# Two pairs of score bursts two gathers later, and one batch's transposes one unit at a step

## The chip, the cores and the metric

The kernel runs on one core of a Trainium2 chip. The metric is the device time of one execution in microseconds. The engines are named as in the profile: PE is TensorE, PEld its weight loads, DVE is VectorE, ACT is ScalarE, POOL is GpSimd and SP is SyncE, which here only issues DMAs.

## What is computed

A talking-heads attention over 8 batches, 12 heads, 448 positions and 64 features a head, and behind it a feed-forward layer with a squared ReLU:

```python
scores = scale * np.matmul(q, k.transpose(0, 1, 3, 2))        # q, k, v: (8, 12, 448, 64)
scores = np.einsum('bhij,hg->bgij', scores, w_pre)             # heads mixed before the softmax
attn = np.exp(scores - np.max(scores, axis=-1, keepdims=True))
attn = attn / (np.sum(attn, axis=-1, keepdims=True) + 1e-09)
attn = np.einsum('bhij,hg->bgij', attn, w_post)                # heads mixed after it
x = np.matmul(attn, v)                                         # to (8*448, 768)
...
h = np.maximum(x @ w_in, 0.0)                                  # w_in: (768, 2048)
out = h * h @ w_out                                            # w_out: (2048, 768)
```

## The kernel before

**Tiles and steps.** A tile is ten query positions of one batch with all twelve heads, 120 rows, by 448 keys. A batch has 45 tiles, so the main loop has 360 steps and a few more at its end; in step `i` the tile `steps[i]` is mixed (`mix`) and the tile four steps back is finished (`unmix`). Step 45 is the first tile of batch 1, step 90 that of batch 2.

**Stages of a tile.** `mix` multiplies the gathered scores G (120 rows) with a matrix that mixes heads (m_ps, L438); ScalarE takes the exponential (e, L442) with its row sums; VectorE takes reciprocals (rc, L449), and GpSimd scales the second mixing matrix with them (pn, L452). `unmix` multiplies e with pn, which also transposes (at_ps, L467 and L471), and VectorE copies the result (at, L473). After every fifteen tiles `av_unit` multiplies with v (ot_ps, L229 and L236). The feed-forward layer of a batch (h_ps at L283, hr, h; o_ps at L328, osb) is cut into units in the list `filler`, and `fill` puts them between the other work so that TensorE has something to do.

**Scores and gathers.** Scores are computed by heads, but a tile needs all heads of ten positions together. So a *burst* (`score_burst`) computes the scores of one *block* of 128 query positions for three of the six head pairs: six matmuls (s_ps, L377) into six PSUM banks, then six copies into a tile `S`, four on ScalarE (L387) and two on VectorE (L389). Two bursts fill a block. `S` has two buffers, which the blocks take in turn. A DMA issued by SyncE (`gather`, L406) then moves the rows of a tile out of S into one of twelve buffers G. Gathers run ten steps ahead of their use. A burst's copies overwrite the block two back, so they wait for the last gather out of that one; a gather waits for the copies of its block.

**When bursts are issued.** `FIRST[b][blk]` is the first tile that counts as block `blk`'s. When the gather of that tile plus n has been issued, and n is in `BURSTS[b][blk]`, one of the two bursts of the *following* block is issued:

```python
first = BURSTS[b2][blk2]
if nxt < len(blocks) and t2 - FIRST[b2][blk2] in first:
    x = first.index(t2 - FIRST[b2][blk2])
    score_burst(*blocks[nxt], [3 * x, 3 * x + 1, 3 * x + 2])
```

`FIRST` is (0, 13, 26, 39) for batches from 1 on. So `BURSTS[1][1]` = [5, 8] places the bursts of batch 1's third block behind the gathers of its tiles 18 and 21, which are issued in steps 53 and 56, and `BURSTS[2][0]` = [5, 8] those of batch 2's second block behind the gathers of its tiles 5 and 8, in steps 85 and 88.

**Transposes.** The next batch's q and k are staged by DMAs and transposed on TensorE. A `turn_unit` transposes two head pairs of q or k: 28 small matmuls (tr_ps, L214) into two PSUM banks and two copies on VectorE (L216). A batch needs three units for k and then three for q; `TURN` gives the step of each, counted from the first step of the batch before.

**What sets the order.** The order on TensorE and GpSimd is that of the program. A scheduler orders VectorE and ScalarE. Every PSUM tile is one of eight banks, taken in turn, so a matmul that opens a tile waits until the tile eight before it has been read. Weights, q, k and v are loaded by DMAs that GpSimd issues at set steps (L89, L250, L254, L267, L273).

Of the kernel before, what the change touches and what calls it, by code (L numbers as in the profile page):

```python
# [14 lines left out]
B, H, S, D = 8, 12, 448, 64  # L15
# [17 lines left out]
BURSTS = {0: ([4, 8], [5, 8])}  # L33
for _b in range(1, B):
    STARTS[_b], FIRST[_b], BURSTS[_b] = (0, 128, 256, 384), (0, 13, 26, 39), ([5, 8], [5, 8], [6], [2, 4])
GATHERS_AT = 2
HALF = H // 2
TT = 15
TQ = TT * IQ
LAG = 4  # L40
AHEAD = 10
SCALE = 1.0 / 8.0
TURN = {0: (21, 21, 21, 25, 25, 25), 1: (24, 24, 24, 28, 28, 28), B: (2 + LAG,) * 3 + (17 + LAG,) * 3}
KQ_LATER = {1: (26, 28, 37, 41), B: (22, 25, 28, 31)}
V_LATER = {1: (30, 32, 34), B: (34, 37, 40)}
KQ_AT = {1: (4, 7, 10, 12), 2: (49, 51, 53, 55)}
# [9 lines left out]
def kernel(  # L56
# [161 lines left out]
    def turn_units(b):  # L218
        return [(250, lambda u=u, w=w: turn_unit(b, w, u)) for w in (1, 0) for u in range(NPAIR // 2)]
# [145 lines left out]
    def score_burst(b, blk, pairs):  # L365

        if (b, blk) not in Sb:
            Sb[(b, blk)] = work.tile([P, H, S], BF16, name="S", tag="S", bufs=2)
        sb = Sb[(b, blk)]
        q0 = STARTS[b][blk]  # L370
        got = []
        for p in pairs:
            for hh in range(2):
                rs = slice(64 * hh, 64 * hh + 64)
                ps = bank("s_ps")
                if blk < 3:
                    nc.tensor.matmul(ps[:, 0:S], lhsT=qTs[b][rs, p, q0:q0 + P], rhs=kTs[b][rs, p, :],  # L377
                                     start=True, stop=True)
                got.append((2 * p + hh, ps))
            for c in range(2 if blk == 3 else 0):  # L380
                for hh in range(2):
                    rs = slice(64 * hh, 64 * hh + 64)
                    nc.tensor.matmul(got[2 * p + hh][1][64 * c:64 * c + 64, 0:S], lhsT=qTs[b][rs, 3 * c + p, q0:S],  # L383
                                     rhs=kTs[b][rs, 3 * c + p, :], start=True, stop=True)
        for h, ps in got:
            if h % 2 == 0 or (b < 3 and h in ((1, 3) if blk == b == 0 else (3, 9))):
                nc.scalar.copy(out=sb[:, h, :], in_=ps[:, 0:S])  # L387
            else:
                nc.vector.tensor_copy(out=sb[:, h, :], in_=ps[:, 0:S])  # L389
# [91 lines left out]
    def at_step(i, unit):  # L481
        timed.setdefault(i, []).append(unit)
# [12 lines left out]
    with tc.manual_schedule(engines={PE, POOL}):  # L495
# [40 lines left out]
        for i in range(-1, end):  # L536
# [9 lines left out]
            if s0:  # L546
                b, t = s0
                if t == 0:
                    if b + 1 < B:
                        for x, u in enumerate(turn_units(b + 1)):  # L550
                            at_step(i + TURN.get(b, TURN[B])[x], u)
            early = [x for x in bounds if x > i]
# [22 lines left out]
            if i < 2:  # L575
                score_burst(0, 0, [2 + 2 * i, 3 + 2 * i])
            for _ in range(2 if i >= GATHERS_AT else 0):
                if ahead[0] > min(max(i + AHEAD, FIRST[0][1] - 1), len(steps) - 1):
# [47 lines left out]
```

## Time and profile before

| | |
|---|---|
| median of three timed runs | 588.79 us (588.3 to 590.7) |
| profiled execution | 584.89 us |
| its span, first to last instruction | 583.1 us |
| granted TensorE clock | 0.999 |
| busy: PE, PEld | 561.5, 362.6 us |
| busy: DVE, ACT, POOL | 398.5, 378.4, 377.7 us |
| DMAs of the gathers (L406 and L409) | 312 and 98 |

Times in the profile count from the first instruction. A row of a timeline gives the start, the length, engine, line, operation, the tile written and those read, the shape and the count; in brackets stands the idle time of the engine before it and what ended that. A row of the waits gives the total, the times and the longest. TensorE's matmuls overlap in the pipeline, so a group's next start is a better measure of its cost than its length.

### The profile page before, as it was taken

The page shows a single profiled execution, that of the slowest core. Times are in us where ns is not written, and L with a number is a line of the kernel's source. Part 1 is how long each engine was busy: PE and PEld are TensorE (multiplying, and loading weights), DVE is VectorE, ACT ScalarE, POOL GpSimd, SP SyncE. Part 2 cuts the span into 40 slices and gives each one's busy share as a digit, 9 for nine tenths or more (in the row PEclk, how much of TensorE's full clock was granted, in tenths as well). Part 3 has the DMA queues.
Part 4 walks back from the last instruction along what each step waited for, and adds up shares of the span by engine and source line. Part 5 has one row for each costly group of instructions (what it writes and reads, how often), then busy time and mean ns, then how long its engine had stood idle before and what let it go on. Part 6 is the DMA issues. An engine that isn't in the chain of part 4 may idle for free.

```text
span 583.1 us, 18427 instructions
## 1 busy us (share of the span) xinstructions
PE 561.5 (96%) x6735; PEld 362.6 (62%) x6735; DVE 398.5 (68%) x979; ACT 378.4 (65%) x1090; POOL 377.7 (65%) x844
## 2 busy tenths in 40 slices
PE   4999989989999999999999999999999999999996
PEld 2677767656566566566565665666665665666554
DVE  7748848868676777866877678767877668655011
ACT  3747968678876567864876558775777548862410
POOL 6566985575877448774778547785578447774830
PEclk9999999999999999999999999999999999999999
DMA  9999999696578764796559855687544865422113
GB/s 130 153 192 172 189 200 180 135 200 161 103 120 148 144 126 89 126 154 141 101 102 140 152 126 97 121 142 157 112 73 69 145 130 101 88 46 55 29 27 82
DMA packets 84043, 72.28 MB, mean 124 GB/s; under 512 B 18768, under 2 KB 80496, under 8 KB 83952
## 3 DMA queue, kind: packets, MB, share of 16 engines
q0 software_dynamic: 37856, 33.04, 36.9%
q1 hardware_dynamic: 45514, 37.86, 30.3%
q8 instruction: 53, 0.87, 0.6%
q10 hardware_dynamic: 582, 0.21, 0.2%
q14 instruction: 38, 0.31, 0.1%
HBM read 47.28 MB, written 11.01 MB: 100 GB/s over the span
## 4 chain that ended last, share of the span: by engine, by line
PE 90%; DMA 4%; ACT 3%; issue 1%; POOL 1%; DVE 1%; ACTq 0%; POOLq 0%; SPq 0%
PE o_ps L328 25%; PE h_ps L283 24%; PE m_ps L438 11%; PE at_ps L467 10%; PE ot_ps L229 5%; PE s_ps L377 5%; PE m_ps L424 4%; DMA G<-S 3%; PE tr_ps L214 2%; PE ot_ps L236 2%; PE at_ps L471 2%; ACT e L442 1%; PE s_ps L383 1%; ACT S L387 1%; DMA kst<-in_k_dram 1%
## 5 line engine op out<-in xcount | busy, mean ns | idle before, releaser
L442 ACT ACTIVATE e<-m_ps 120x448 bf16<-120x448 f32 x360 | 196.0, 551 | 85.2 <-PE m_ps L438 46.2
L473 DVE CAST at<-at_ps 128x480 bf16<-128x480 f32 (+1 forms) x360 | 206.2, 592 | 63.4 <-PE at_ps L471 48.1
L452 POOL TENSOR_SCALAR pn<-post,rc 120x120 bf16<-120x120 bf16 (+1 forms) x340 | 122.1, 369 | 142.4 <-DVE rc L449 77.1
L283 PE MATMUL h_ps<-xt,w 128*128 128x448 bf16 (+2 forms) x960 | 165.8, 315 | 0.4 <-ACT e L442 0.2
L328 PE MATMUL o_ps<-w,h 128*128 128x384 bf16 x768 | 138.7, 326 | 0.1
L438 PE MATMUL m_ps<-G,pre 120*120 120x448 bf16 (+1 forms) x340 | 121.4, 358 | 4.1 <-ACT S L387 3.0
L467 PE MATMUL at_ps<-pn,e 120*128 120x120 bf16 x1080 | 115.8, 216 | 2.7 <-ACT S L387 2.5
L283 PEld LDWEIGHTS <-w 128*128 128x128 bf16 x960 | 83.4, 98 | 53.4 <-issue 4.2
L467 PEld LDWEIGHTS <-e 120*128 120x128 bf16 x1080 | 85.9, 98 | 47.4 <-ACT S L387 5.1
L295 POOL TENSOR_TENSOR h<-hr 128x384 bf16<-128x384 f32 (+1 forms) x128 | 103.0, 805 | 12.9 <-ACT hr L289 11.4
L328 PEld LDWEIGHTS <-h 128*128 128x128 bf16 x768 | 73.0, 98 | 47.9 <-issue 4.9
L289 ACT ACTIVATE hr<-h_ps 128x448 f32<-128x448 f32 (+2 forms) x136 | 71.9, 530 | 44.8 <-PE h_ps L283 37.3
L387 ACT CAST S<-s_ps 128x448 bf16<-128x448 f32 x177 | 82.2, 550 | 14.6 <-PE s_ps L377 9.2
L389 DVE CAST S<-s_ps 128x448 bf16<-128x448 f32 x141 | 79.8, 614 | 4.8 <-DMA G<-S 4.0
L442 ACT ACTIVATION_READ_ACCUMULATOR e<-m_ps 120x1 f32 x360 | 75.6, 210 | 0.0
L337 DVE COPY osb<-o_ps 128x384 f32<-128x384 f32 x54 | 30.1, 557 | 57.8 <-PE o_ps L328 57.6
L449 DVE RECIPROCAL rc<-sm 120x1 f32<-120x1 f32 (+1 forms) x192 | 31.1, 162 | 42.3 <-ACT e L442 30.9
L438 PEld LDWEIGHTS <-pre 120*120 120x120 bf16 (+1 forms) x340 | 44.9, 132 | 21.4 <-issue 12.3
L242 ACT CAST xt<-ot_ps 128x450 bf16<-128x450 f32 (+1 forms) x48 | 25.6, 534 | 26.5 <-PE ot_ps L236 26.0
L455 POOL TENSOR_TENSOR en<-e,rc 120x128 bf16<-120x128 bf16 (+1 forms) x112 | 42.3, 378 | 0.0
L229 PE MATMUL ot_ps<-at,v 128*64 128x150 bf16 x864 | 41.5, 229 | 0.0
L471 PE MATMUL at_ps<-post,en 120*128 120x120 bf16 x181 | 39.1, 216 | 0.0
(63 smaller groups left out, 494.6 us busy)
## 6 DMA issues: line engine op xcount, KB each, us to landing
G<-S SPq DMA_DIRECT2D x276, 105.0 KB
out_dram<-osb POOLq DMA_DIRECT2D x48, 192.0 KB, 4.5
kst<-in_k_dram POOLq DMA_DIRECT2D x14, 336.0 KB, 7.3
qst<-in_q_dram POOLq DMA_DIRECT2D x14, 336.0 KB, 5.7
G<-S SPq DMA_DIRECT2D x70, 52.5 KB
v<-in_v_dram POOLq DMA_DIRECT2D x8, 384.0 KB, 8.6
w<-in_moe_w_in_dram POOLq DMA_DIRECT2D x6, 512.0 KB, 10.3
w<-in_moe_w_out_dram POOLq DMA_DIRECT2D x8, 384.0 KB, 8.7
```

The costliest lines, as they stand in the source:

```text
L229: nc.tensor.matmul(ps[64 * hh:64 * hh + 64, TQ * y:TQ * y + TQ], lhsT=vts[b % 2][:, g, r, :], rhs=at[:, r, g, :, :].rearrange("p t i -> p ...
L283: nc.tensor.matmul(ps[:, n * j:n * j + n], lhsT=w1[f // 8][:, c2, f % 8 * 128:f % 8 * 128 + 128], rhs=xts[b][:, c2, n0:n1], start=(c2 == 0 ...
L289: nc.scalar.activation(out=hr[:, 0:k * n], in_=ps[:, 0:k * n], func=ACT.Relu)
L295: eng.tensor_tensor(out=dst[:, :, x - o:y - o], in0=hr[:, :, x - n0:y - n0], in1=hr[:, :, x - n0:y - n0], op=ALU.mult)
L328: nc.tensor.matmul(ps[:, 0:384], lhsT=lhsT, rhs=w2[ft // 4][:, ft % 4, nt * 384:(nt + 1) * 384], start=(ft == 0), stop=(ft == FT - 1))
L387: nc.scalar.copy(out=sb[:, h, :], in_=ps[:, 0:S])
L389: nc.vector.tensor_copy(out=sb[:, h, :], in_=ps[:, 0:S])
L438: nc.tensor.matmul(ps[0:n, 0:S], lhsT=m[0:n, 0:n], rhs=Gs.pop(s)[0:n, :], start=True, stop=True)
L442: nc.scalar.activation(out=e[0:n, x, :], in_=ps[0:n, 0:S], func=ACT.Exp, scale=SCALE, accum_out=sm[0:n, x:x + 1])
L452: nc.gpsimd.tensor_scalar(out=esb[(b, t - z)][1][0:rows, :], in0=(post_gi if fused else post)[0:rows, :], scalar1=rc[0:rows, z:z + 1], sca ...
L467: nc.tensor.matmul(ps[:, RG * r:RG * r + RG], lhsT=e[0:n, tl % 2, P * r:P * r + P], rhs=pn[0:n, :], start=True, stop=True)
L473: nc.vector.tensor_copy(out=ats[(b, third)][:, 0:k, :, tl, :], in_=ps[:, 0:k * RG].rearrange("p (r g i) -> p r g i", r=k, i=IQ))
```

## The change

Three entries of tables change; no operation is added or removed.

```diff
 for _b in range(1, B):
     STARTS[_b], FIRST[_b], BURSTS[_b] = (0, 128, 256, 384), (0, 13, 26, 39), ([5, 8], [5, 8], [6], [2, 4])
+BURSTS[1] = ([5, 8], [7, 10], [6], [2, 4])
+BURSTS[2] = ([7, 10], [5, 8], [6], [2, 4])
...
-TURN = {0: (21, 21, 21, 25, 25, 25), 1: (24, 24, 24, 28, 28, 28), B: (2 + LAG,) * 3 + (17 + LAG,) * 3}
+TURN = {0: (20, 22, 23, 24, 26, 27), 1: (24, 24, 24, 28, 28, 28), B: (2 + LAG,) * 3 + (17 + LAG,) * 3}
```

The bursts of batch 1's third block move behind the gathers of tiles 20 and 23 (steps 55 and 58), and those of batch 2's second block behind the gathers of tiles 7 and 10 (steps 87 and 90). The six transposing units of batch 1, which stood three by three in steps 21 and 25, go one each into steps 20, 22, 23, 24, 26 and 27. The two added lines shift every later line by two: L438 before is L440 after. The feed-forward units, which fill what is left of each step, move by a unit here and there in steps 20 to 27; from batch 2's third block on the order on every engine is as before, and GpSimd's and SyncE's orders are as before throughout.

## The prediction

> **What bounds the kernel now.** I read the first part of the page, then the windows, then the chain and the waits, and last the timelines of TensorE around each wait that the change can reach.
>
> ```profile
> PE 561.5 (96%) x6735; PEld 362.6 (62%) x6735; DVE 398.5 (68%) x979; ACT 378.4 (65%) x1090; POOL 377.7 (65%) x844
> ...
> DMA  9999999696578764796559855687544865422113
> ...
> PE 90%; DMA 4%; ACT 3%; issue 1%; POOL 1%; DVE 1%; ACTq 0%; POOLq 0%; SPq 0%
> ```
> ```profile
> 48.00:54.00 6.00, 4.89 (x132) 3.92 (x131) 5.20 (x18) 3.69 (x14) 3.60 (x9) 1.00 0.84 170
> 84.00:90.00 6.00, 3.37 (x42) 2.42 (x42) 2.52 (x7) 2.80 (x8) 5.01 (x11) 1.00 1.33 197
> 90.00:104.00 14.00, 14.00 (x205) 11.06 (x203) 11.76 (x37) 11.69 (x39) 7.26 (x19) 1.00 0.84 175
> ```
> ```profile
> 240.00:300.00 60.00, 59.68 (x747) 37.77 (x746) 44.38 (x107) 41.12 (x119) 43.31 (x99) 1.00 0.69 125
> 480.00:540.00 60.00, 60.00 (x652) 38.72 (x650) 38.91 (x93) 38.18 (x111) 38.78 (x89) 1.00 0.38 74
> ```
> The columns of a window are length, then busy us of TensorE, its weight loads, VectorE, ScalarE and GpSimd, then granted clock, DMA share and GB/s. TensorE is busy 561.5 of 583.1 us and carries 90% of the chain. From 240 us on it fills its windows (59.68 and 60.00 of 60), and the next engine, VectorE, has 15 us to spare in one of them. So a microsecond of TensorE idling that goes in the first 140 us should arrive whole at the end, unless something takes it back before then. The DMA row is what could: up to 102 us (seven slices of 14.6 us) the DMA engines are busy nine tenths or more. All of the change lies inside the first 140 us.
>
> ```profile
> ACT S L387 <- DMA G<-S: 5.4, 2, 3.2
> ...
> DVE S L389 <- DMA G<-S: 4.0, 2, 2.9
> ```
> In the list of waits (total, times, longest) the two copies out of score bursts wait for gathers, twice each. A burst's copies write an S buffer of which there are two, so they cannot start before the last gather out of the block two back has landed. Both waits are at bursts that the change moves.
>
> **Part one: batch 1, the burst for its third block.** TensorE's timeline (start, length, what), with the chain's own account of the release:
>
> ```profile
> 83.94 0.74 PE L377 MATMUL s_ps<-kT,qT 64*128 64x448 bf16 x6
> 84.62 0.94 PE L283 MATMUL h_ps<-xt,w 128*128 128x148 bf16 x12
> 85.40 0.35 PE L438 MATMUL m_ps<-G,pre 120*120 120x448 bf16 x1
> 88.28 0.33 PE L467 MATMUL at_ps<-pn,e 120*128 120x120 bf16 x3 [2.53 <-ACT S L387]
> ...
> 89.48 0.35 PE L438 MATMUL m_ps<-G,pre 120*120 120x448 bf16 x1
> 89.67 0.93 PE L283 MATMUL h_ps<-xt,w 128*128 128x148 bf16 x12
> ...
> 90.66 0.35 PE L438 MATMUL m_ps<-G,pre 120*120 120x448 bf16 x1
> ...
> 91.88 0.74 PE L377 MATMUL s_ps<-kT,qT 64*128 64x448 bf16 x6
> 92.55 0.40 PE L438 MATMUL m_ps<-G,pre 120*120 120x448 bf16 x1
> ...
> 95.05 0.94 PE L283 MATMUL h_ps<-xt,w 128*128 128x148 bf16 x12
> ...
> 100.20 0.35 PE L438 MATMUL m_ps<-G,pre 120*120 120x448 bf16 x1
> ```
> ```profile
> 86.33 1.25 DMA G<-S
> 87.69 0.11 ACT S L387
> ```
> Six score matmuls take six of the eight PSUM banks at 83.94. ScalarE and VectorE stand before their copies until a gather has landed at 86.33 + 1.25 = 87.58 us, and TensorE runs out of banks: 2.53 us idle. By the order of the built program the changed kernel does two more steps first, and the burst stands just ahead of the m_ps that was at 90.66. What comes before it, from 83.94 on: the h_ps group (85.40 - 84.62 = 0.78), the m_ps of 85.40 (0.19 to the next start, as from 89.48 to 89.67), and all from 88.28 to 90.66 (2.38), 3.35 together. So the burst comes at 87.3; its first score matmuls are done when the gather lands at 87.6. The stall is then 0 to 0.3 us, and TensorE is ahead by up to 2.53.
>
> What is late next is a gather. While the loads of weights and of batch 2 are under way, gathers land at their own pace:
>
> ```profile
> 79.48 0.40 PE L438 MATMUL m_ps<-G,pre 120*120 120x448 bf16 x1 [0.79 <-DMA G<-S]
> ```
> ```profile
> 84.01 16.62 SPq L406 DMA_DIRECT2D G<-S  x14
> ```
> ```profile
> SPq L406 <- DMA G<-S: 10.5, 15, 1.4
> ```
> The m_ps at 79.48 (tile 5 of batch 1) found its gather only just landed. SyncE issued 14 gathers in 16.62 us, 1.19 us each, and stood 10.5 us between 70 and 100 us before gathers that had not landed; I take that pace for the landings. Tile 20 then lands at 79.48 + 15 x 1.19 = 97.3. It was used at 100.20, the eleventh m_ps from 89.48 on. 2.53 earlier would be 97.67: only 0.4 to spare, with an error in the pace of 0.05 us being 0.75. If all the gap stays, 2.53; if gathers are as late as the worst wait here (0.79 twice over), about 1.0. I take 2.0. The range of this term is 0 (the copies wait at the new place just as long) to 2.53.
> [...]
>
> The second burst moves from the gather of tile 21 to that of tile 23. It stood at 91.88 and now stands ahead of the h_ps that was at 95.05. That place comes earlier by the stall, 2.53, and by its own 0.67 (92.55 - 91.88): 91.85, as before. So the third block is full when it was, and its gathers, which queue behind that in SyncE, start when they did.
>
> **Part two: batch 2, the burst for its second block.**
>
> ```profile
> 127.91 0.74 PE L377 MATMUL s_ps<-kT,qT 64*128 64x448 bf16 x6
> 130.25 0.35 PE L438 MATMUL m_ps<-G,pre 120*120 120x448 bf16 x1 [1.59 <-ACT S L387]
> 131.08 1.47 PE L328 MATMUL o_ps<-w,h 128*128 128x384 bf16 x8
> ...
> 139.35 0.35 PE L438 MATMUL m_ps<-G,pre 120*120 120x448 bf16 x1
> ```
> ```profile
> 129.66 0.54 ACT S L387
> ```
> ```profile
> L89 POOL DMA_DIRECT2D qst<-in_q_dram x2: 698/706/715, 124.2 to 130.1; - x2
> ...
> DMA to landing us min/median/max: 8.1/8.3/8.5
> ```
> The same picture: the copies start at 129.66 and TensorE idles 1.59. In the new order two m_ps and two at_ps groups (130.25 to 131.08, 0.83) go first, then the burst, then o_ps (1.3 us). The burst comes at 127.91 + 0.83 = 128.7, its copies at 129.66 as before, and the m_ps after o_ps needs a bank at 128.7 + 0.7 + 1.3 = 130.7, when the first copy (0.54) has ended. The 1.59 goes. What is late next: the q load issued at 130.1 lands near 138.4 by its 8.3 us, and a gather issued beside it serves the m_ps that stood at 139.35 (tile 6); 1.59 earlier it would want its gather at 137.76, up to 0.6 before that load is out of the way. So 1.0 to 1.6; I take 1.0, the range being 0 to 1.59.
>
> **Part three: the transposes of batch 1.**
>
> ```profile
> 44.18 1.04 PE L214 MATMUL tr_ps<-ident,kst 64*64 64x64 bf16 x84
> 48.66 0.92 PE L214 MATMUL tr_ps<-ident,qst 64*64 64x64 bf16 x57
> 49.91 0.28 PE L214 MATMUL tr_ps<-ident,qst 64*64 64x64 bf16 x11 [0.34 <-ACT e L442]
> 50.97 0.32 PE L214 MATMUL tr_ps<-ident,qst 64*64 64x64 bf16 x16 [0.78 <-issue]
> ```
> ```profile
> L473 DVE CAST at<-at_ps 128x480 bf16<-128x480 f32 (+1 forms) x360 | 206.2, 592 | 63.4 <-PE at_ps L471 48.1
> ```
> ```profile
> 50.05 1.98 DVE L216 COPY qT<-tr_ps 128x448 bf16<-128x448 bf16 x6
> ```
> Three units in a row take six banks; the second row of three lacks banks twice, 0.34 + 0.78 = 1.12 us. One by one, 28 transposes (0.33 us) and two copies (1.98 / 6 = 0.33 each) come per step, and the work is the same. But VectorE is the busiest after TensorE here, 5.20 of 6.00 us, with the same copies still to do, so not all can go; and the last q unit now comes at step 27, where the burst for batch 1 reads it. Between them stand one h_ps group (0.78) and an at_ps group (0.4): 1.2 us, against two copies of 0.33 behind a reciprocal that waits for an exponential. From -0.5 (each of six units waits 0.27 us, which gives back 1.6) to 1.12; I take 0.4, since VectorE's 0.8 idle us in that window limit it. The weight loads queue behind steps 27 on and move with it, so the gathers up to 79.48 move too.
>
> **The sum.** 0.4 + 2.0 + 1.0 = 3.4 us. The profiled execution took 584.89 us, 1.8 beyond its span, so 581.5; the median of the three timed runs, 588.79, is 3.9 us above it, and the same microseconds taken off it give 585.4, -0.58%. A run of this kernel tells about 0.5% (2.9 us) from no change, so the forecast lies just beyond that line.
>
> **The rivals.**
> *The gathers take it back* (0.20). While the DMA engines are full the next gathers become the wait: part one gives 0.8, part two 0.4, part three nothing: 587.6. For it: 1.33 of DMA share in 84 to 90 us, and the spare 0.4 us at tile 20. Against it: 0.84 in the window after, so the queue is emptying.
> *All of it arrives* (0.07): 1.12 + 2.53 + 1.59 = 5.2, 583.6. Against it: VectorE at 5.20 of 6.00 and the 0.4 us.
> *Slower: the single units make TensorE wait for VectorE* (0.08). Each unit needs two banks, and its copies queue behind reciprocals and casts. Where each of six units loses two copies and a cast (2 x 0.33 + 0.59, 1.2 us), that is 7.2; less the 1.12 removed and the 3.0 of the bursts, 3.1 us slower, 591.9. It decides from (3.0 + 1.12) / 6 = 0.7 us per unit on. For it: TensorE idled 0.78 at one unit. Against it: the first row of three, at 44.18, went through without a wait.
> *TensorE is not the bound later* (0.03). Its idle time would be made up by another engine's pace behind 140 us: 588.8. [...] The two late windows, with VectorE at 44.38 of 60, speak against it.
>
> **How the numbers follow.** The forecast has 0.62, of which 0.48 lies beyond 2.9 us of gain and 0.14 short of it; its own range is a gain of 1.5 to 4.6 (584.2 to 587.3). Faster: 0.48 + 0.07 = 0.55. Same: 0.14 + 0.20 + 0.03 = 0.37. Slower: 0.08. The range reaches from a gain of 4.9 (583.9) to none (588.9, rounded up), which takes in the first and last rivals and leaves out the other two.
>
> **What would show it.** Right: no idle time of ScalarE or VectorE before S copies longer than 0.5 us; TensorE without the 2.53 and the 1.59; a new gather wait under 0.8 us near tile 20 of batch 1; tr_ps without idle time. Wrong: an idle TensorE before s_ps at step 27, gather waits of over 1 us between 90 and 100 or near 138 us, or the S copies waiting again at their new place.

## The result, and the profile after

| | before | after |
|---|---|---|
| median of ten timed runs | 588.75 us (587.97 to 591.81) | 586.45 us (584.11 to 588.94) |
| ratio | | 0.9954, 95% interval 0.9932 to 0.9976 |
| profiled execution, its span | 584.89, 583.1 us | 587.93, 586.1 us |

The change saves 2.3 us of medians; by the ratio 0.46%, between 0.24% and 0.68%. The two profiled executions say the opposite, 3.0 us slower after. Both are single executions, and why they fall so is half of the answer. Of the 3.0 us, 1.06 are a later start-up (there already at tile 20 of batch 0), 0.7 come at one place in batch 6 (shown with the transposes below), and the rest is what a new wait, shown in the next views, costs beyond the change's gain.

The page of the kernel after, its busy times and the shares of the chain that ended last:

```profile
PE 565.5 (96%) x6735; PEld 363.3 (62%) x6735; DVE 399.0 (68%) x979; ACT 379.2 (65%) x1090; POOL 377.8 (64%) x844
...
PE 89%; DMA 6%; ACT 2%; POOL 1%; DVE 1%; issue 1%; SPq 0%; ACTq 0%; POOLq 0%
```

TensorE is busy 4.0 us longer than the 561.5 of before with the same 6735 instructions: part of them ran at a lower clock (0.996 in the mean against 0.999), about 1.7 us of it, as an estimate, in the window of half clock shown below. DMA has gone from 4% to 6% of the chain.

TensorE's timeline after, around the bursts of part one:

```profile
80.21 0.32 PE L469 MATMUL at_ps<-pn,e 120*128 120x120 bf16 x3 [1.12 <-POOL pn L454]
80.79 0.40 PE L440 MATMUL m_ps<-G,pre 120*120 120x448 bf16 x1 [0.27 <-DMA G<-S]
...
87.99 0.94 PE L379 MATMUL s_ps<-kT,qT 64*128 64x448 bf16 x6
88.89 0.37 PE L440 MATMUL m_ps<-G,pre 120*120 120x448 bf16 x1
...
92.63 0.74 PE L379 MATMUL s_ps<-kT,qT 64*128 64x448 bf16 x6
```
```profile
99.71 0.40 PE L440 MATMUL m_ps<-G,pre 120*120 120x448 bf16 x1 [0.77 <-DMA G<-S]
```

The 2.53 us ahead of at_ps are gone. In their place stands a wait of 0.77 us for the gather of tile 20, as forecast. Around the bursts of part two nothing is idle either:

```profile
130.61 1.47 PE L330 MATMUL o_ps<-w,h 128*128 128x384 bf16 x8
...
132.97 1.15 PE L379 MATMUL s_ps<-kT,qT 64*128 64x448 bf16 x6
```

But a third place, which the change does not touch, has a wait that was not there before. First the waits of after between 107 and 134 us (total, times, longest), then its TensorE and its ScalarE, then the same place before:

```profile
ACT S L389 <- DMA G<-S: 4.1, 1, 4.1
DVE S L391 <- DMA G<-S: 3.8, 1, 3.8
...
PE m_ps L440 <- ACT S L389: 2.8, 1, 2.8
```
```profile
114.77 1.56 PE L379 MATMUL s_ps<-kT,qT 64*128 64x448 bf16 x6
116.26 1.47 PE L330 MATMUL o_ps<-w,h 128*128 128x384 bf16 x8
120.58 0.48 PE L440 MATMUL m_ps<-G,pre 120*120 120x448 bf16 x1 [2.85 <-ACT S L389]
```
```profile
120.00 1.84 ACT L389 CAST S<-s_ps 128x448 bf16<-128x448 f32 x4 [4.07 <-DMA G<-S]
```
```profile
115.06 1.28 PE L377 MATMUL s_ps<-kT,qT 64*128 64x448 bf16 x6
116.27 1.47 PE L328 MATMUL o_ps<-w,h 128*128 128x384 bf16 x8
117.58 0.35 PE L438 MATMUL m_ps<-G,pre 120*120 120x448 bf16 x1
```
```profile
115.82 1.84 ACT L387 CAST S<-s_ps 128x448 bf16<-128x448 f32 x4
```

This is the first burst of batch 2's first block. It overwrites the third block of batch 1, whose last rows go out with the gather of tile 38. After, its copies start at 120.00 because that gather lands only then; before, they followed their matmuls at 115.82. The windows of after (length, busy of TensorE, its weight loads, VectorE, ScalarE, GpSimd, then granted clock, DMA share, GB/s) show what follows:

```profile
117.25:120.67 3.42, 0.57 (x5) 0.32 (x3) 0.60 (x2) 0.67 (x2) 1.28 (x3) 1.00 1.23 203
120.67:124.08 3.41, 3.41 (x18) 1.48 (x18) 3.07 (x8) 3.41 (x11) 1.06 (x3) 0.50 1.21 190
124.08:134.00 9.92, 9.92 (x130) 6.75 (x128) 6.15 (x16) 7.03 (x23) 6.35 (x15) 1.00 0.87 138
```

For 3.41 us behind the wait, from 120.67 on, TensorE is granted half its clock (0.50); half of that stretch, 1.7 us, is an estimate of what this costs more.

### The profile page after: what moved, and what is told of

The parts are those of the page before. It is cut to its first block, busy times and chain, and to the rows that moved or that the text cites. A ratio compares the mean times of both kernels' runs of the same rounds, so it can differ in the third digit from the quotient of the medians.

```text
span 586.1 us, 18430 instructions
## 1 busy us (share of the span) xinstructions
PE 565.5 (96%) x6735; PEld 363.3 (62%) x6735; DVE 399.0 (68%) x979; ACT 379.2 (65%) x1090; POOL 377.8 (64%) x844
## 4 chain that ended last, share of the span: by engine, by line
PE 89%; DMA 6%; ACT 2%; POOL 1%; DVE 1%; issue 1%; SPq 0%; ACTq 0%; POOLq 0%
PE o_ps L330 24%; PE h_ps L285 23%; PE m_ps L440 11%; PE at_ps L469 10%; PE ot_ps L231 5%; DMA G<-S 5%; PE s_ps L379 5%; PE m_ps L426 4%; PE tr_ps L216 2%; PE ot_ps L238 2%; PE at_ps L473 2%; PE s_ps L385 1%; ACT S L389 1%; DMA kst<-in_k_dram 1%; POOL qst L91 1%
## 5 line engine op out<-in xcount | busy, mean ns | idle before, releaser
L440 PE MATMUL m_ps<-G,pre 120*120 120x448 bf16 (+1 forms) x340 | 122.1, 360 | 5.6 <-ACT S L389 4.3
L440 PEld LDWEIGHTS <-pre 120*120 120x120 bf16 (+1 forms) x340 | 45.1, 133 | 21.4 <-issue 11.0
L379 PE MATMUL s_ps<-kT,qT 64*128 64x448 bf16 x276 | 39.3, 363 | 0.3
```

Source lines behind the costliest of these rows:

```text
L440: nc.tensor.matmul(ps[0:n, 0:S], lhsT=m[0:n, 0:n], rhs=Gs.pop(s)[0:n, :], start=True, stop=True)
```

## The experiments

The theory at the start: the change removes its three waits, and the new wait near 120 with its half clock takes most of it back. Open were whether part one makes that wait, why, and why the times are better than the profile all the same. In the kernels of the experiments the added entries stand on an existing line, so line numbers are those of before. Medians and ratios are against runs of the kernel before on the same chip in the same series: 589.75 us for the first four kernels, 589.35 for the next four, 589.30 for the last four.

**The transposes alone.**

```diff
-TURN = {0: (21, 21, 21, 25, 25, 25), 1: (24, 24, 24, 28, 28, 28), B: (2 + LAG,) * 3 + (17 + LAG,) * 3}
+TURN = {0: (20, 22, 23, 24, 26, 27), 1: (24, 24, 24, 28, 28, 28), B: (2 + LAG,) * 3 + (17 + LAG,) * 3}
```

> Only the table of transposing units is changed (20, 22, 23, 24, 26, 27). Theory A (each part removes its own wait and most of it arrives): the 1.12 us of idle time at tr_ps is gone, TensorE reaches step 32 some 0.7 us earlier counted from step 20, and the median falls by 0.5 to 0.7 us. Rival B (in batch 1 the gathers set the pace): the 0.7 us is lost again as gather waits by tile 9 of batch 1, and the median is unchanged within 0.3 us. The 2.5 us before at_ps and the 1.6 us in batch 2 stay in both.

Measured: 589.03 us, 0.9986 (0.9964 to 1.0007). The idle time at tr_ps is gone, and from step 20 to step 32 TensorE gains 0.38 us on a second profile of before (below), where the transposes had waited 0.75 us, and 0.72 on the first one, where they had waited 1.12. The waits for copies of scores at 90.44 (2.38 us) and 134.60 (2.31 us) stay, and the burst near 120 does not wait. A gain of 0.8 us by the ratio, with an interval that includes none: the size of the term is borne out by the trace, not by the times.

The profile has a later loss that offsets it. At tile 8 of batch 6, between 413 and 419 us, TensorE stands idle where it does not in either profile of before. The same place in before, and in the whole change:

```profile
413.04 0.32 PE L467 MATMUL at_ps<-pn,e 120*128 120x120 bf16 x3
```
```profile
416.17 0.33 PE L469 MATMUL at_ps<-pn,e 120*128 120x120 bf16 x3 [0.66 <-DVE at L475]
```

Against before, 0.9 us is lost there in this kernel, 0.7 and 0.9 in the two profiles of the whole change, and 0.6 to 1.4 in six of the kernels below; the kernels with one pair of bursts alone and the one with batch 2's first bursts one gather later lose nothing. Why a kernel has this loss stays open: the order of the instructions is the same there, and the profile's releaser fits badly, since with the transposes alone TensorE goes on only 0.3 us after that copy has ended.

**Batch 1's bursts alone.**

```diff
+BURSTS[1] = ([5, 8], [7, 10], [6], [2, 4])
```

> Only the bursts of batch 1's third block are moved. Theory A: the wait of 2.5 us is gone, gather waits near tiles 17 to 21 bring back at most 0.7, the median falls by 1.8 to 2.5 us. Rival B (gathers set the pace up to 104 us): gather waits bring back 1.5 us or more, TensorE is under 1 us ahead at tile 24 of batch 1, and the median falls by under 1 us. Rival C (the first burst of batch 2, three gathers after the last one out of its buffer, now waits instead): ScalarE stands before S copies near 115 to 120 us for over 1 us, and the median falls by nothing or rises.

Measured: 588.84 us, 0.9978 (0.9957 to 0.9998). TensorE's timeline:

```profile
99.28 0.40 PE L438 MATMUL m_ps<-G,pre 120*120 120x448 bf16 x1 [0.85 <-DMA G<-S]
120.51 0.53 PE L438 MATMUL m_ps<-G,pre 120*120 120x448 bf16 x1 [3.64 <-ACT S L387]
133.00 0.35 PE L438 MATMUL m_ps<-G,pre 120*120 120x448 bf16 x1 [0.24 <-ACT S L387]
```

Part one by itself brings the wait near 120, so the rival by which batch 2's first burst waits instead holds. It also shortens part two's wait to 0.24 us without moving those bursts: TensorE, held up near 120, reaches the burst near 130 later, and by then its gather has landed.

**Batch 2's bursts alone.**

```diff
+BURSTS[2] = ([7, 10], [5, 8], [6], [2, 4])
```

> Only the bursts of batch 2's second block are moved. Theory A: the wait of ScalarE for a gather near 129 us is gone, and gather waits near tile 6 of batch 2 bring back up to 0.6: the median falls by 1.0 to 1.6 us. Rival B: the copies wait as long at the new place, and the median is unchanged within 0.3 us. The 2.5 us in batch 1 stays in both.

Measured: 586.75 us, 0.9936 (0.9916 to 0.9956), from six runs. The wait near 90 is there (3.55 us), none is near 120 or 130, and the gathers of batch 2's first tiles now make TensorE wait 0.68 us at 136.32. The gain, 3.0 us of medians, is more than the 1.59 us of wait that the change removes. The half clock that such a wait can bring is the candidate, not shown: the granted clock is 0.998 in the mean of these runs and 0.9954 in those of before, but six runs are few, and with the transposes added (the last kernel below) the gain is smaller.

**The whole change a second time.** No edit.

> The whole change once more, for a second profile. Theory A: the median is 2 to 2.5 us below before, and the 2.85 us of idle time that the first profile shows before the m_ps at 120.58, with a granted clock of 0.83 behind it, is a chance event of that execution: it is absent or under 1 us here, and the span is 584.5 or less. Rival C: the first burst of batch 2 waits in every execution of the changed kernel, over 2 us here too, with the lower clock behind it.

Measured: 587.97 us, 0.9953 (0.9931 to 0.9975), the same as the first time. The profile has the wait near 120 again, 2.61 us, and the half clock behind it (0.50 for 3.41 us from 122.95 on), so it is no chance event of the first profile, and rival C holds here too. The parts alone sum to 0.0100; the whole has 0.0047. They do not add: the gap, 0.0053, is just beyond the 0.0042 that the four intervals together leave, as an estimate.

**The kernel before a second time.**

```diff
-GATHERS_AT = 2
+GATHERS_AT = 1 + 1
```

> The kernel before, profiled a second time (one constant is written as a sum, nothing else). Theory A, half clock: the profile shown of before (584.89 us, 3.9 us under its median) is an execution in which the clock did not drop behind TensorE's waits of 2.53 us (before at_ps, near 88) and 1.59 us (before m_ps, near 130), and the usual execution loses 1.7 us or twice that to a half clock of 3.41 us behind one or both. Then this profile has the same two waits on the copies of scores, at least one half-clock stretch of 3.41 us within 3 us behind one of them, a granted clock of 0.991 to 0.997, and 587 to 590 us. Rival B: the profile shown is typical and executions differ only in how late the first loads arrive: the two waits are there, no stretch of half clock but in the tail, clock 0.998, and the span differs from 583.1 by the delay at the first gathered tile (within 1 us). In neither does the first burst of batch 2's first block wait for its gather: tile 38's first gather of batch 1 is issued ahead of the k load of batch 3 and lands 3.5 us later.

Measured: 587.99 us in its one run. The waits are at the same places, 2.81 and 1.49 us, and the clock fell behind the first of them: 0.50 for 3.41 us, from 91.49 on. The windows are this stretch with the 3.42 us ahead of it, and then three as long around the two waits of the first profile of before:

```profile
88.07:91.49 3.42, 1.56 (x21) 1.35 (x22) 1.64 (x4) 2.24 (x6) 1.22 (x3) 1.00 1.24 209
91.49:94.90 3.41, 3.41 (x30) 3.18 (x28) 2.62 (x8) 2.31 (x8) 1.17 (x3) 0.50 0.97 186
```
```profile
83.91:87.32 3.41, 1.84 (x21) 1.07 (x19) 0.91 (x3) 0.58 (x3) 3.37 (x7) 1.00 1.41 196
87.32:90.73 3.41, 2.35 (x33) 2.14 (x34) 2.15 (x6) 3.04 (x9) 1.73 (x5) 1.00 1.23 204
128.28:131.69 3.41, 1.82 (x17) 1.15 (x14) 2.35 (x5) 2.03 (x5) 2.50 (x6) 1.00 0.90 225
```

The second fence is the execution that the prediction was made from. TensorE is idle 1.57 us in its first window, 1.06 in the next (together the wait of 2.53 us and 0.1 of another) and 1.59 in the third, and the clock stays at 1.00 there and up to 580 us. In the second profile of before TensorE is idle 1.86 us in the 3.42 us ahead of the half clock. Why the clock fell in one execution and not in the other is not shown. Theory A holds: the profile shown of before is an execution without that loss. It is 3.1 us shorter in span than this one. Of that, 0.2 are there at the start of batch 1, 1.1 come between 80 and 84 us, where gathers are waited for, 0.3 are the longer wait for the copies, and 1.5 come in the window of half clock. The last figure can be read off the same instructions, first in this profile, then in the one that the prediction was made from, where the at_ps behind the wait starts at 88.28:

```profile
89.83 0.33 PE L467 MATMUL at_ps<-pn,e 120*128 120x120 bf16 x3 [2.81 <-ACT S L387]
...
95.97 0.94 PE L283 MATMUL h_ps<-xt,w 128*128 128x148 bf16 x12
```
```profile
92.95 0.93 PE L283 MATMUL h_ps<-xt,w 128*128 128x148 bf16 x12
```

The same work with no wait in it takes 6.14 us here and 4.67 there. The transposes alone have 0.50 for 3.41 us three times in one execution, with 1.42, 2.28 and 1.97 us of idle TensorE in the 3.41 us ahead:

```profile
78.02:81.43 3.41, 1.99 (x28) 1.21 (x27) 1.49 (x4) 2.10 (x7) 3.38 (x8) 1.00 1.04 231
81.43:84.84 3.41, 3.41 (x63) 3.11 (x59) 0.38 (x2) 1.48 (x4) 3.38 (x7) 0.50 1.26 188
88.26:91.67 3.41, 1.13 (x16) 1.02 (x17) 1.59 (x3) 1.82 (x5) 1.17 (x3) 1.00 1.22 197
91.67:95.08 3.41, 3.41 (x28) 2.96 (x26) 2.23 (x8) 2.72 (x10) 1.09 (x3) 0.50 0.98 184
132.63:136.04 3.41, 1.44 (x13) 1.03 (x13) 1.95 (x4) 2.03 (x5) 1.78 (x5) 1.00 0.88 240
136.04:139.45 3.41, 3.41 (x17) 1.39 (x15) 2.12 (x5) 2.16 (x8) 1.07 (x3) 0.50 0.90 169
```

A stretch of 0.50 also stands behind TensorE's wait of 3.64 us near 120 with batch 1's bursts alone (from 120.30 on) and behind the one of 3.55 us near 90 with batch 2's alone (from 91.48 on), each 3.41 us long.

**The loads of batch 3 later, with the whole change.**

```diff
-KQ_LATER = {1: (26, 28, 37, 41), B: (22, 25, 28, 31)}
+KQ_LATER = {1: (35, 36, 38, 41), B: (22, 25, 28, 31)}
```

> The whole change, and the loads of q and k for batch 3 are issued at steps 35, 36, 38 and 41 of batch 1 instead of 26, 28, 37 and 41, behind tile 38's gathers. Theory A, the queued gather: the 2.6 to 3.6 us that TensorE waits near 120 for the first burst of batch 2's first block come from tile 38's first gather being issued 0.3 to 0.8 us behind the k load (landing 7.8 to 8.5 us later) instead of 0.9 us ahead of it (3.5 us later). Then that gather lands 3.4 to 5 us behind its issue, the copies of that burst start within 1 us of its matmuls, the wait and the half clock behind it are gone, 4.3 us in all, and the time is 1.5 to 5 us under the whole change: ratio to before 0.987 to 0.993. Rival B, pace: the gathers of the third block are late by themselves since the burst ahead of them was moved; the lag stays at 7 us or more without the load, the wait stays at 2 us or more, ratio 0.994 to 0.997. Rival C: the wait only moves to where the loads are now (steps 36 to 44 and the first tiles of batch 2): TensorE waits over 2 us between 122 and 140, ratio 0.993 to 0.998.

Measured: 587.46 us, 0.9965 (0.9939 to 0.9991). The first gather of tile 38 lands 5.25 us behind its issue, the copies start at 116.53, the wait near 120 is gone, and the granted clock is 1.00 in every window from 96 to 160 us:

```profile
116.53 1.84 ACT L387 CAST S<-s_ps 128x448 bf16<-128x448 f32 x4 [1.08 <-DMA G<-S]
```

But the loads now stand before batch 2's first tiles:

```profile
136.94 0.40 PE L438 MATMUL m_ps<-G,pre 120*120 120x448 bf16 x1 [0.80 <-DMA G<-S]
139.74 0.40 PE L438 MATMUL m_ps<-G,pre 120*120 120x448 bf16 x1 [0.47 <-DMA G<-S]
141.18 0.40 PE L438 MATMUL m_ps<-G,pre 120*120 120x448 bf16 x1 [0.89 <-DMA G<-S]
```

TensorE is 4.6 us ahead of the second profile of before at batch 2's first tile and 1.25 at its tile 8; about 0.8 of the difference is order, since the moved second burst now comes behind that first tile. Theory A holds for the wait, rival C for the time: 2.2 us of waits for gathers, spread over three places.

**The same loads later in the kernel before**, as a control, with the same line of diff on the kernel before.

> The kernel before with only the later loads of q and k for batch 3 (steps 35, 36, 38 and 41 of batch 1), as a control. Theory A: in the kernel before, tile 38's first gather is ahead of the k load anyway (issue 110.55 against 111.44) and the burst behind it doesn't wait, so the loads' place is worth nothing there: ratio 0.998 to 1.002, waits of 2 to 3.6 us near 88 to 90 and of 1.5 to 2.5 us near 130 to 135 as before. Rival B: the loads slow the gathers generally and moving them helps by itself: 0.990 to 0.996. Rival C: they are now later than batch 3 needs or collide with the loads of v at steps 30 to 34 and the first gathers of batch 2: 1.003 or more.

Measured: 588.87 us, 0.9988 (0.9964 to 1.0012), waits of 2.49 us near 89 and 1.18 us near 132: no effect by itself that the times show, as theory A has it. Its profile does lose 1.4 us in batch 6, which the kernel before does not, so a gain of about that size could be hidden here.

**Batch 2's first bursts one gather later, with the whole change.**

```diff
-BURSTS[1] = ([5, 8], [7, 10], [6], [2, 4])
+BURSTS[1] = ([5, 8], [7, 10], [6], [3, 5])
```

> The whole change, and the two bursts for batch 2's first block one gather later (behind the gathers of tiles 42 and 44 instead of 41 and 43 of batch 1). Theory A: the first burst's six score matmuls then run near 116.3 instead of 114.8, tile 38's gather still lands near 120, so TensorE's wait near 120 shrinks from 2.85 us by 1 to 1.7 us to between 1.1 and 1.9 us, which is short of the 2.3 us behind which the clock was seen to drop (6 of 7 times): the half clock goes too, 1.5 to 3 us in all under the whole change, ratio to before 0.989 to 0.993. Rival B: the wait is set by the copies and not by the landing, and moves with the burst: 2.5 us or more near 122, ratio 0.994 to 0.997. Rival C: the second burst is now late for the first gathers of batch 2 and TensorE waits for G in the first tiles of batch 2 (over 2 us near 136 to 142): ratio 0.995 to 1.001.

Measured: 587.12 us, 0.9971 (0.9942 to 1.0). The wait near 120 falls to 1.40 us, and the clock stays at 1.00 around it, as theory A has it:

```profile
116.53:119.95 3.42, 2.02 (x18) 1.13 (x17) 2.15 (x6) 1.48 (x5) 3.34 (x9) 1.00 1.00 199
119.95:123.36 3.41, 3.09 (x24) 1.59 (x22) 2.21 (x6) 3.29 (x10) 1.96 (x5) 1.00 1.42 206
```

The gather of batch 2's tile 3 comes 1.36 us late at 138.52 instead. The ratio fell short of its 0.989 to 0.993; it lies in the range of rival C, whose waits for gathers are there in kind, but smaller than its 2 us.

**The loads just behind tile 38's gather**, with the whole change.

```diff
-KQ_LATER = {1: (26, 28, 37, 41), B: (22, 25, 28, 31)}
+KQ_LATER = {1: (30, 31, 37, 41), B: (22, 25, 28, 31)}
```

> The whole change, and the first two of batch 3's four q and k loads are issued at steps 30 and 31 of batch 1 instead of 26 and 28: just behind tile 38's gathers, not ten steps behind as in the run with steps 35 to 41. Theory A, queued gather: tile 38's first gather lands 3.4 to 5.5 us behind its issue, TensorE's wait near 120 for the scores of batch 2's first block is under 0.5 us and the half clock there goes. Theory D, a stretch bound by DMA: TensorE still starts tile 8 of batch 2 at 144.5 to 146 us, since the gathers of batch 2's tiles 3 to 6 land at 138.5 to 142 whatever TensorE's lead is (four loads less in the way now than there: waits for G of 0.5 to 2.5 us in all near 132 to 141). By A with D: ratio to before 0.993 to 0.997, no better than the whole change by more than 0.002. By A without D: 0.987 to 0.992.

Measured: 586.40 us, 0.9951 (0.9929 to 0.9973). The gather lands 5.1 us behind its issue, the copies start at 115.73, no wait near 120 and no half clock in the profile (1.000 in the mean); 0.87 us of wait for a gather at 139.53. Tile 8 of batch 2 starts at 143.0 us, better than theory D's 144.5; still, of a lead of 5.3 us at the first tile (against the second profile of before, about 0.8 of it order again) 2.9 are left at tile 8. The time is what "A with D" gave.

**v of batch 2 earlier**, with the whole change.

```diff
-V_LATER = {1: (30, 32, 34), B: (34, 37, 40)}
+V_LATER = {1: (20, 22, 24), B: (34, 37, 40)}
```

> The whole change, and the three loads of batch 2's v are issued at steps 20, 22 and 24 of batch 1 (near 103 to 108 us, DMA share 0.55) instead of 30, 32 and 34 (near 116 to 124 us, DMA share 1.0 to 1.2). Nothing else: the k load stays ahead of tile 38's gather. Theory A: the wait of 2.6 to 3.6 us near 120 for the first burst of batch 2's first block stays at 2 us or more, since the v loads were issued behind that gather, and the half clock behind it stays in most executions. Theory D: v is 768 KB, 4 us at the 180 GB/s of this stretch, so the gathers of batch 2's tiles 0 to 6 land 2 to 4 us sooner; alone this gains little (TensorE waits near 120 anyway), ratio 0.993 to 0.997. Rival E: the v loads delay the third block's gathers of batch 1 (tiles 26 to 38, issued from 95 to 112): TensorE waits for G between 105 and 118, ratio 0.997 or more.

Measured: 587.20 us, 0.998 (0.9956 to 1.0004). A miss for theory A: in this profile tile 38's gather was issued 0.7 us ahead of the k load, not behind it, and the wait near 120 did not occur. Rival E's waits for gathers between 105 and 118 are not there either, so the profile, which caught the fastest of the twelve executions, gives no cause for the worse ratio, whose interval overlaps the whole change's. What it does show is how narrow the order is: it falls one way or the other by under a microsecond.

**Both edits of loads**, with the whole change.

```diff
-KQ_LATER = {1: (26, 28, 37, 41), B: (22, 25, 28, 31)}
-V_LATER = {1: (30, 32, 34), B: (34, 37, 40)}
+KQ_LATER = {1: (30, 31, 37, 41), B: (22, 25, 28, 31)}
+V_LATER = {1: (20, 22, 24), B: (34, 37, 40)}
```

> The whole change with both edits: v of batch 2 at steps 20, 22, 24 and the first q and k loads of batch 3 at steps 30 and 31 of batch 1. Theory A with D: the first takes the k load out of the way of tile 38's gather, the second takes 4 us of DMA out of the stretch that bounds batch 2's first gathers, and only both together pass TensorE's lead on: no wait over 1 us near 120, waits for G under 1 us in all from 130 to 142, tile 8 of batch 2 at 141.5 to 143.5 us (start-up as in the second profile of before), ratio to before 0.988 to 0.993. Rival F, no stretch bound by DMA: the lead is lost elsewhere (gathers paced by their issue, eight in flight), tile 8 at 144.5 or later, ratio 0.993 to 0.997. Rival E as for the v loads alone: waits for G from 105 to 118, 0.997 or more.

Measured: 585.99 us, 0.9954 (0.9931 to 0.9977). No wait near 120, 0.72 us for a gather at 139.80, a new wait of 1.46 us at a transpose at 112.56, half clock once (0.50 for 3.41 us from 81.30 on), behind small waits that added to 1.42 us between 77.89 and 81.30. Tile 8 at 143.8, just outside the 141.5 to 143.5 of A with D; the ratio is that of rival F. It does not beat the whole change.

**The whole change without batch 1's bursts.**

```diff
-BURSTS[1] = ([5, 8], [7, 10], [6], [2, 4])
 BURSTS[2] = ([7, 10], [5, 8], [6], [2, 4])
```

> The change without the moved bursts of batch 1: batch 2's bursts at gathers 7 and 10 and the single transposes. Told of the parts so far: batch 1's bursts alone 0.9978, batch 2's alone 0.9936 (6 runs), the transposes alone 0.9986, all three 0.9954. If batch 1's bursts are worth nothing inside the whole (what TensorE gains near 88 it waits for near 120), this runs at 0.992 to 0.996, with the wait of 2.4 to 3.6 us near 90 and the half clock behind it, no wait near 120, none near 130. If batch 1's bursts carry the gain, 0.997 to 1.000. If they cost time inside the whole, 0.988 to 0.992.

Measured: 586.50 us, 0.9959 (0.9932 to 0.9986). The wait near 90 is there, 3.30 us, and the clock is 0.50 from 87.33 to 94.16; nothing waits near 120 or 130. This is the first of the three cases: batch 1's bursts are worth nothing that can be measured inside the whole. By the two intervals, a worth of less than about 2 us would not be seen.

**The order that makes the wait.** For every profile with the point at issue: by how much the first gather of tile 38 was issued behind batch 3's k load (negative: ahead), its time to landing, and TensorE's wait for the burst, in us. A landing is the last update of the gather's semaphore ahead of that semaphore's next use, in the traces.

| kernel | behind the k load | to landing | wait near 120 |
|---|---|---|---|
| before, twice; transposes; batch 2's bursts; these two | -0.88 to -0.89 | 3.5 | 0 |
| before, loads later | load 12 later | 3.5 | 0 |
| after | 0.76 | 7.8 | 2.85 |
| after, second time | 0.31 | 8.1 | 2.61 |
| batch 1's bursts alone | 0.65 | 8.5 | 3.64 |
| after, bursts one later | 0.46 | 6.7 | 1.40 |
| after, v earlier | -0.69 | 6.2 | 0 |
| after, loads at 35 or 30, or with v earlier | load 5 to 12 later | 5.1 to 6.1 | 0 |

GpSimd's timeline before, and then after, has the load:

```profile
111.44 0.70 POOL L89 DMA_DIRECT2D kst<-in_k_dram  x1
```
```profile
111.16 0.70 POOL L91 DMA_DIRECT2D kst<-in_k_dram  x1
```

and the gather was issued at 110.55 before and 111.92 after. Start-up was 1.06 us later in this execution of after; without that the gather is issued 0.3 us later than before and the load 1.3 us earlier. Two stores of 192 KB, issued just behind the load, move up with it: the first stands 1.6 us behind the gather before, and 0.06 us ahead of it after.

**Where the times come from.** Over the 93 runs of before that were timed beside the experiments the granted clock is 0.9956 in the mean, over the 22 runs of the whole change it is 0.9980 (start and tail are in both). The difference, 0.0024 of 588 us, is 1.4 us, as an estimate. Among runs with 0.998 or more, 13 of 93 and 13 of 22, the medians are 587.09 and 585.67, again 1.4. So about half of the gain is waiting time that is gone, and half is clock that no longer drops behind it. This splits the times by a quantity that was not set by any experiment, so it is a reading of them rather than a test.

## Why the prediction was right, and where not

The direction, the range and nearly the size held: 586.45 against 585.4, 2.3 us of gain against 3.4, on the near side of the 0.5% line where the forecast lay just beyond it. The working behind the sum was right at the change's own places and wrong about what lies around them.

- *Part one, the place.* The burst was to come at 87.3 and the second at 91.85; they came at 87.99 and 92.63, 0.7 to 0.8 us later in an execution whose start-up was 1.06 later. The 2.53 went, and the new wait at tile 20 was 0.77, where the sum had taken 0.5 and under 0.8 was the sign of being right. This working held.
- *Part one, the term.* 2.0 was taken; inside the whole no worth of it can be measured (0.9954 with it, 0.9959 without). The step that failed is what that part drew from its last sentence, that the gathers "start when they did" and so nothing more is lost. They did, within 0.3 us, and that was the trouble. GpSimd issues the k load at its step, and with TensorE ahead the step came, start-up apart, 1.3 us sooner, and the gather was issued 0.3 us later; SyncE, which issues it, stood before gathers that had not landed for 11.7 us between 70 and 105 us before, and for 12.9 after. So the load overtook the gather, which then took 7.8 us instead of 3.5 and held up a burst two blocks on. By this, the first of the prediction's own signs of being right failed: ScalarE stood 4.07 us before S copies, where at most 0.5 was to be. The prediction asked what is late next among the gathers that TensorE needs, and not which gather frees a buffer.
- *Part two.* The 1.59 went, with a gather wait behind it as said (0.68 us at 136.32 in the run of that part alone, against up to 0.6). The term of 1.0 was too small by the run alone, 3.8 us (2.6 to 5.0) by its ratio; the clock that fell behind this wait in the profile of the transposes alone (0.50 from 136.04 to 139.45) was not in it, and whether it makes up the rest is not shown. In the whole it had less to remove: held up near 120, TensorE with batch 1's bursts alone met only 0.24 there.
- *Part three.* 0.4 by VectorE's room; 0.38 to 0.72 from step 20 to 32. Of what it gained, part was waited for again at 80.21 (1.12 us for pn), and in the kernel of this part alone 0.9 us went in batch 6.
- *The sum.* The prediction read its waits in an execution 3.9 us faster than the median and took their 3.4 us off the median, as if the same stalls cost the same in both. They do not: the second profile of before has a half clock of 3.41 us behind the first of them, which cost 1.5 us more, and the profiled execution was one in which the clock had not dropped. That half clock is the missing term, and it made up for what was lost near 120. That the sum came so near is in part luck: a loss and a gain that it did not have offset each other.
- *The rivals.* "The gathers take it back" was right in kind; it came as a buffer that is freed late and, once that is mended, as waits for gathers in batch 2's first tiles (2.2 us with the loads at 35, 0.87 at 30). "Slower" by single units did not occur: tr_ps shows no wait. "TensorE is not the bound later" is out: from batch 2's tile 8 on every kernel keeps its lead to within 0.45 us up to the start of batch 6, and behind the loss of up to 1.4 us at tile 8 of batch 6 again to the end.
- *The pace of the gathers.* The prediction took the gathers to land at a pace of their own beside the loads, 1.19 us each by its reading of 84 to 101 us. Near 112 the trace does not show such a pace: a gather of 42 KB issued 0.76 us behind a load of 336 KB landed at 119.75, behind it (117.92).

What is not settled: why tile 38's gather still takes 5.1 to 6.2 us in the kernels with part one when the k load is not ahead of it, and whether the share of 1.0 to 1.4 of the DMA engines between 116 and 124 us is the limit by itself; moving v out of it gave no measurable time. A candidate for the first that no run tests is the two stores: the first was issued 0.03 to 0.32 us ahead of that gather in the three kernels with later loads, and 1.0 to 1.6 us behind it wherever it took 3.5 us. With v alone earlier, the last load of v stood 1.6 us ahead instead.

## What to carry to other kernels

When a stall goes, list what is issued in program order by an engine that follows the freed one, and what is paced by its own landings: here the first moved up by 1.3 us, the second did not (0.3 us later), and the load overtook a gather whose landing frees a buffer (7.8 us to landing instead of 3.5). Weigh a wait of TensorE by more than its length where the profiles show a lower clock behind it (1.5 us more in the one comparison here), and compare several profiles of the same kernel before taking one execution's stalls for the usual ones. Parts tested alone can overstate a change when each hides the other's wait.

## What the runs showed of the hardware

In the one place that could be compared, a wait of TensorE with a lower granted clock behind it cost 1.5 us more than its length: in the second profile of before the clock was 0.50 for 3.41 us behind a wait of 2.81 us, and the work behind that wait took 6.14 us, against 4.67 in the first profile, where the clock stayed at 1.00 behind a wait of 2.53 us. In the first profile of the whole change it was 0.50 for 3.41 us behind a wait of 2.85 us; with batch 2's first bursts one gather later it stayed at 1.00 behind one of 1.40 us. What decides whether the clock falls is not shown by these runs.
